# Reordering the prologue of a fused attention and mixer kernel: centroids on ScalarE's queue, argmax ahead of a low part, another low part on GpSimd

## The chip, the cores and the metric

One core of a Trainium2 chip runs the whole program. The metric is the device time of that core in microseconds, the median of the runs shown. The engines are TensorE (PE, with its weight loads PEld), VectorE (DVE), ScalarE (ACT), GpSimd (POOL) and SyncE (SP), which here only issues transfers.

## The reference

The input q, k and v have 2 batches of 8 heads with 768 tokens of 64 values; each head has 16 centroids. Every token of q and of k is assigned to the centroid with the largest product (the first one, if several are equal), and a token attends only to the tokens of its own cluster. Two feed-forward mixers follow.

```python
q_assign = np.argmax(np.einsum('bhsd,hcd->bhsc', q_n, c_n), axis=-1)
k_assign = np.argmax(np.einsum('bhsd,hcd->bhsc', k_n, c_n), axis=-1)
mask = q_assign[:, :, :, None] == k_assign[:, :, None, :]
scores = np.where(mask, scale * np.matmul(q, k.transpose(0, 1, 3, 2)), -1e9)
attn = softmax(scores)
x = np.matmul(attn, v)            # heads joined to (2, 768, 512)
k = np.maximum(xk @ w_k, 0.0)     # xk, xr: x mixed with the token before
x = sigmoid(xr @ w_r) * (k * k @ w_v)
u = x + (np.maximum(x.T @ w_tok1, 0.0) @ w_tok2).T
out = u + np.maximum(u @ w_ch1, 0.0) @ w_ch2
```

## The kernel before, in words

The heads are worked in 8 pairs (2 batches of 4 pairs); head 0 and head 1 below are the two heads of the first pair. For each pair, `loads` (L614) brings q and k of both heads, transposed and doubled over the partitions, in four transfers into four temporary tiles `t0` to `t3`; they are used in turn, so a load of the next pair overwrites the tile that the pair before held in its place. A product is made from two numbers for each value: a high part, rounded to the engine's format (`hi`, L642), and a low part, the value less its high part (`lo`, L650). `hi(e, 0)` and `hi(e, 1)` write the high parts of q and k of head e into `qa` and `ka` on ScalarE; `hi(e, 2)` writes the high part of k once more into `kb`, on GpSimd; `lo(e, 0)` writes the low part of q into `qb` and `lo(e, 1)` the low part of k into the lower half of `ka`. The score of a block of 128 tokens (`score`, L826) is a sum of two parts: part 0 from `qa` and `ka`, and part 1 from `qb` and `kb`. Rows 64 to 79 of `qb` and `kb` hold the cluster mask.

The mask is made so: the centroids are loaded (`cr`, L939), squared and summed on ScalarE (L947), normalised by a chain of small operations on GpSimd and VectorE, transposed on TensorE and copied to `cn` (L967). For the first pair, `sims_head(e)` (L671) forms the similarities of one head on TensorE from `cn` and the raw q and k, `sime_head` (L698) copies them out on ScalarE, `simt_head` (L681) transposes them on TensorE, `first_max(e)` (L738) finds the argmax in five steps on VectorE (L743, L744, L747, L750 and L691, which writes the one-hot rows `oh`), `mask_first` (L771) transposes `oh` on TensorE, and `mask_evac` (L776) writes the mask rows, for q on VectorE (L780) and for k on ScalarE (L782). Then part 1 of the first scores can run, then the row maximum (L844, VectorE), the exponential (L853, ScalarE), transposes and products with v.

Each engine has a queue of its own and executes it in the order in which the program writes the instructions; semaphores between the queues are put in by the framework. Three things set the order around the change. The prologue from L937 to L969 is written out by hand: constants, centroids, loads, and then the branch `n == 0` of `prep_steps` (L784 to L808), whose lines stand in the order in which their instructions are issued. The list that it returns (`first`) holds the steps of the first pair that are left to the planner: `lo(1, 1)` and `hi(1, 2)` on GpSimd, `lo(1, 0)` and the second argmax on VectorE, and others. From there on a planner (`run_plan`, L997) orders the attention of all 8 pairs: each operation has an engine, an assumed duration, its dependencies and a due time; for each engine the ready operation with the smallest sum of start time and 0.29 of the due time is next. Due times come from `want` (L1053), which adds a multiple of a period to `T_FIRST`, the time at which the steady order is assumed to begin; the planner's clocks of the engines start from the same constant:

```python
def want(n, key, j=0.0):
    return T_FIRST + PER * (n + (EARLY.get(n, LATE.get(n - NP, {})).get(key, DUE[key]) + j) / NTASK)

now.update(P=T_FIRST + 0.75, A=T_FIRST + 0.5, D=T_FIRST + 0.65, G=T_FIRST - 2, S=T_FIRST - 6)
```

The planner runs while the program is built; nothing of it is measured at run time. After the attention the mixers run with TensorE as the engine that most work waits for, their weights converted on VectorE and ScalarE beside it.

Of the kernel before, what the change touches and what calls it, by code (L numbers as in the profile page):

```python
# [50 lines left out]
MM512 = 0.2265  # L51
GSTEPS = 18
PER = 23.929
T_FIRST = 11.753
CROSS = 0.117
LAND = 2.1
SWITCH = 0.122
# [241 lines left out]
def f32(ap):  # L299
    return ap.bitcast(F32)  # L300
# [3 lines left out]
def cluster_attention_moe_mixer(ctx: ExitStack, tc, q, k, v, cent, mu_k, mu_r, w_k, w_v, w_r, w1, w2, wc1, wc2, out):  # L304
    nc = tc.nc
# [44 lines left out]
    class Chain:  # L350
# [14 lines left out]
        def step(self, n=1):  # L365
            for _ in range(n):
                e, us, two = self.op[:3]
                t = self.start() + us
                now[e] = t
                if e == "G":  # L370
                    lock[1] = t
                elif two:
                    lock[0] = t
                self.ready = t + LAT
                self.count += 1
                self.op = next(self.gen, None)
                if self.op is None:
                    self.done = True
                    pipe.remove(self)
                    return  # L380
                if len(self.op) > 3:
                    self.due = self.op[3]
# [214 lines left out]
    with ExitStack() as actx:  # L597
# [8 lines left out]
        def copy(eng, dst, src):  # L606
            if eng == "D":
                nc.vector.tensor_copy(dst, src)
            elif eng == "A":
                nc.scalar.activation(dst, src, AF.Copy)  # L610
            else:
                nc.gpsimd.tensor_copy(dst, src)
# [16 lines left out]
        def prep_steps(n):  # L629
# [12 lines left out]
            def hi(e, w):  # L642
                qa, qb, ka, kb = stks[n]
                dst, src = ((qa[:, e], qr[e]), (ka[:, e], kr[e]), (kb[0:D, e], kr[e][0:D]))[w]
                if w == 2 and n and ENG["hi2"] == "S":
                    nc.sync.dma_start(out=f32(dst), in_=f32(ka[0:D, e]))
                else:
                    copy(ENG[f"hi{w}"], dst, src)

            def lo(e, w, eng=None):  # L650
                eng = eng or (nc.vector if ENG[f"lo{w}"] == "D" else nc.gpsimd)
                qa, qb, ka, kb = stks[n]
                if w == 0:
                    dst, src, h = qb[0:D, e], qr[e][0:D], qa[0:D, e]
                else:
                    dst, src, h = ka[D:P, e], kr[e][D:P], ka[D:P, e]
                eng.tensor_tensor(out=dst, in0=src, in1=f32(h), op=ALU.subtract)
# [13 lines left out]
            def sims_head(e):  # L671
                st["ps", e] = ps = banks8[:, (6, 5)[e], 0:HS]
                for hf in range(2):
                    for j, r in ((0, qr), (1, kr)):
                        o = 32 * (2 * hf + j)
                        nc.tensor.matmul(
                            ps[o : o + 32, :], cn[0:D, 2 * p + e, :], r[e][0:D, hf * HS : (hf + 1) * HS],
                            start=True, stop=True,
                        )

            def simt_head(e):  # L681
                ps = banks8[:, (6, 4)[e], 0:HS].rearrange("p (h i a b) -> p h i a b", h=2, i=HT, b=32)
                for i in range(HT):
                    nc.tensor.transpose(
                        ps[:, :, i].rearrange("p h a b -> p h (a b)"), st["sm", e][:, i * P : (i + 1) * P], ident
                    )
                groups = ps.rearrange("p h i a b -> p (h i a) b")
                st["sv", e], st["eq", e] = groups[:, :, 0:NC], groups[:, :, NC:]

            def aoh_head(e):  # L690
                nc.vector.tensor_tensor(  # L691
                    out=ohs.rearrange("p h i a b -> p (h i) a b")[:, :, 2 * e : 2 * e + 2, 0:NC],
                    in0=st["rk", e].rearrange("p (g a) b -> p g a b", a=2),
                    in1=st["m2", e].rearrange("p (g a) -> p g a", a=2).unsqueeze(3).to_broadcast([P, NT, 2, NC]),
                    op=ALU.is_equal,
                )

            def sime_head(e):  # L698
                if e == 0:
                    st["sm"] = sml.tile([P, S], F32, tag="sm", bufs=1, name="sm")  # L700
                st["sm", e] = sm = st["sm"][:, e * HS : (e + 1) * HS]
                nc.scalar.activation(sm, st["ps", e], AF.Copy)
# [35 lines left out]
            def first_max(e):  # L738
                mx = sml.tile([P, HT * 4], F32, tag=f"mx{e}", bufs=1, name="mx")
                st["m2", e] = m2 = sml.tile([P, HT * 4], F32, tag=f"m2{e}", bufs=1, name="m2")  # L740
                st["rk", e] = rk = st["eq", e]
                return [
                    lambda: nc.vector.tensor_reduce(mx, st["sv", e], axis=AX.X, op=ALU.max),  # L743
                    lambda: nc.vector.tensor_tensor(  # L744
                        out=rk, in0=st["sv", e], in1=mx.unsqueeze(2).to_broadcast([P, HT * 4, NC]), op=ALU.is_ge
                    ),
                    lambda: nc.vector.tensor_tensor(  # L747
                        out=rk, in0=rk, in1=rank.unsqueeze(1).to_broadcast([P, HT * 4, NC]), op=ALU.mult
                    ),
                    lambda: nc.vector.tensor_reduce(m2, rk, axis=AX.X, op=ALU.max),  # L750
                    lambda: aoh_head(e),
                ]
# [18 lines left out]
            def mask_first(j, e, at):  # L771
                ps = st["pf", j] = banks8[:, at].bitcast(BF16)[:, 0:S]
                for i in range(NT):
                    nc.tensor.transpose(ps[D : D + 32, i * P : (i + 1) * P], oh[i // HT][:, i % HT, 2 * e + j], identb)
# [8 lines left out]

            alloc()  # L784
            if n == 0:
                hi(0, 0), hi(0, 1)
                sims_head(0)
                fill(FILL[1])
                lo(0, 1, nc.vector)
                sime_head(0), simt_head(0)  # L790
                lo(0, 0, nc.vector)
                sims_head(1)
                hi(1, 1), sime_head(1), hi(1, 0)
                for step in first_max(0):
                    step()
                for i, t in enumerate(tasks[0:2]):
                    score(t, 0, at=2 * i)
                simt_head(1)
                hi(0, 2)
                mask_first(1, 0, 6), mask_first(0, 0, 7)  # L800
                mask_evac(0, 1, 0, S), mask_evac(0, 0, 0, HS)
                return [
                    lambda: lo(1, 1), lambda: lo(1, 0, nc.vector), lambda: hi(1, 2),
                    first_max(1),
                    lambda at: mask_first(0, 1, at), lambda at: mask_first(1, 1, at),
                    lambda: mask_evac(1, 0, 0, HS), lambda: mask_evac(1, 0, HS, S), lambda: mask_evac(1, 1, 0, S),
                    lambda: mask_evac(0, 0, HS, S),
                ]  # L808
# [17 lines left out]
        def score(t, part=None, at=None):  # L826
            n, hf, i, e = t
            qa, qb, ka, kb = stks[n]
            c0 = (hf * HT + i) * P
            if t not in PS_:  # L830
                PS_[t] = banks8[:, at : at + 2]
            ps = PS_[t]
            parts = ((qa, ka, True), (qb[0 : D + NC], kb[0 : D + NC], False))
            for x, y, first in parts if part is None else parts[part : part + 1]:
                for nh in range(2):
                    nc.tensor.matmul(  # L836
                        ps[:, nh, 0:HS], x[:, e, c0 : c0 + P], y[:, e, nh * HS : (nh + 1) * HS],
                        start=first, stop=not first,
                    )
# [96 lines left out]

        cr2 = sml.tile([P, 2, D], F32, tag="cr", bufs=1, name="cr")  # L937
        cr = cr2[:, 0]
        nc.sync.dma_start(cr, cent)  # L939
        loads(0)  # L940
        load_v(0)
        warm = banks8[:, 4, 0:P]
# [19 lines left out]
        def fill(count):  # L962
            for _ in range(count):
                nc.tensor.transpose(warm, ident, ident)

        fill(FILL[0])
        nc.vector.tensor_copy(cn[:, :, 0:NC], pc.rearrange("p (h c) -> p h c", h=H))  # L967

        first = prep_steps(0)  # L969

        NP = len(pairs)
# [81 lines left out]
# [4 lines that stand above are left out]
        prep, score_, max_, exp_, turn_, tp_, ev_, move_, pv_, xe_, parts, load_, mask_dma, load_v_ = ({} for _ in range(14))  # L1057
# [529 lines left out]
```

## Time and profile before

| | us |
|---|---|
| median of 3 runs | 621.73 |
| lowest and highest run | 620.47, 622.57 |
| the profiled execution | 621.98 |
| its span | 620.2 |
| TensorE busy | 606.2 (98%) |
| VectorE busy | 477.2 (77%) |
| ScalarE busy | 356.1 (57%) |
| GpSimd busy | 128.5 (21%) |

The span runs from the first to the last instruction of the profiled execution; the device time has 1.8 us more around it. Busy times are sums over the span, so an engine that is idle half of the time can still be the one that all others wait for in a stretch. The chain of waits goes back from the last instruction: at each step to what released it, or to the instruction before it on its engine; "issue" in it is time in which the engine waited for nothing that the profile shows. The granted clock of TensorE was 0.999 of its full speed.

### The profile page before, as it was taken

The page shows a single profiled execution, that of the slowest core. Times are in us where ns is not written, and L with a number is a line of the kernel's source. Part 1 is how long each engine was busy: PE and PEld are TensorE (multiplying, and loading weights), DVE is VectorE, ACT ScalarE, POOL GpSimd, SP SyncE. Part 2 cuts the span into 40 slices and gives each one's busy share as a digit, 9 for nine tenths or more (in the row PEclk, how much of TensorE's full clock was granted, in tenths as well). Part 3 has the DMA queues.
Part 4 walks back from the last instruction along what each step waited for, and adds up shares of the span by engine and source line. Part 5 has one row for each costly group of instructions (what it writes and reads, how often), then busy time and mean ns, then how long its engine had stood idle before and what let it go on. Part 6 is the DMA issues. An engine that isn't in the chain of part 4 may idle for free.

```text
span 620.2 us, 9514 instructions
## 1 busy us (share of the span) xinstructions
PE 606.2 (98%) x3357; PEld 499.1 (80%) x3357; DVE 477.2 (77%) x850; ACT 356.1 (57%) x677; POOL 128.5 (21%) x181
## 2 busy tenths in 40 slices
PE   8899999999999999999999999999999999999997
PEld 6765757668678568899999998889999899999996
DVE  5999899899898858899869888968986726774113
ACT  4988888889878667967656666134432512332010
POOL 4455744836622541000000000020002000000000
PEclk9999999999999999999999999999999999999999
DMA  8167758659536341344204334143447203300002
GB/s 299 60 203 197 185 172 247 180 177 284 152 90 178 96 137 57 106 136 150 85 0 134 120 121 135 34 103 102 137 137 166 82 23 134 105 34 1 0 2 101
DMA packets 36736, 75.43 MB, mean 122 GB/s; under 512 B 6033, under 2 KB 19345, under 8 KB 36689
## 3 DMA queue, kind: packets, MB, share of 16 engines
q1 hardware_dynamic: 34256, 67.36, 35.9%
q0 software_dynamic: 2432, 7.47, 5.0%
q8 instruction: 26, 0.43, 0.3%
q14 instruction: 22, 0.17, 0.1%
HBM read 48.27 MB, written 3.15 MB: 83 GB/s over the span
## 4 chain that ended last, share of the span: by engine, by line
PE 80%; DVE 9%; DMA 4%; ACT 2%; SPq 2%; issue 2%; POOL 1%; ACTq 0%; DVEq 0%
PE ps L1333 25%; PE ps L1357 24%; PE ps L836 9%; PE ps L925 9%; PE ps L590 5%; PE ps L909 3%; DVE junk L844 3%; DMA uperm<-ublk 2%; DMA t<-k_dram 2%; SPq L1455 1%; PE ps L1413 1%; PE ps L1496 1%; DVE ut L1468 1%; PE ps L666 1%; DVE ublk L1438 1%
## 5 line engine op out<-in xcount | busy, mean ns | idle before, releaser
L1357 PE MATMUL ps<-wu,hl 128*128 128x512 f32 x720 | 170.5, 391 | 0.0
L1357 PEld LDWEIGHTS ps<-wu,hl 128*128 128x128 f32 x720 | 134.6, 188 | 26.8
L1333 PE MATMUL ps<-ut,wu 128*128 128x384 f32 x576 | 104.5, 336 | 0.9 <-DVE ut L1468 0.5
L1333 PEld LDWEIGHTS ps<-ut,wu 128*128 128x128 f32 x576 | 100.9, 188 | 3.5 <-DVE ut L1468 1.0
L844 DVE TENSOR_SCALAR_CACHE_REDUCE junk<-ps 128x768 bf16<-128x768 f32 x96 | 90.1, 938 | 9.3 <-PE ps L836 5.2
L853 ACT ACTIVATE e<-ps,nm 128x768 f32<-128x768 f32 x96 | 86.6, 904 | 18.4 <-DVE junk L844 17.1
L1312 ACT ACTIVATE hl<-ps 128x384 fp32r<-128x384 f32 x48 | 23.4, 490 | 93.8 <-PE ps L1333 93.7
L1314 DVE SCALAR_TENSOR_TENSOR hl<-ps,hl 128x384 fp32r<-128x384 f32 x48 | 26.8, 557 | 60.0 <-ACT hl L1312 59.7
L480 ACT ACTIVATE wu<-g 128x512 fp32r<-128x512 f32 x62 | 39.0, 629 | 56.2 <-DVE g L476 56.1
L1333 PE MATMUL ps<-xmix,wu 128*128 128x384 f32 x384 | 69.7, 336 | 0.7 <-ACT wu L480 0.5
L1333 PEld LDWEIGHTS ps<-xmix,wu 128*128 128x128 f32 x384 | 67.3, 188 | 2.4 <-ACT wu L480 0.8
L836 PE MATMUL ps<-ka,qa 128*128 128x384 f32 x192 | 57.7, 380 | 1.6 <-DVE oh L733 0.8
L1455 POOL DMA_DIRECT2D uperm<-ublk x16 | 7.9, 499 | 228.9 <-ACT h L1400 168.3
L836 PE MATMUL ps<-kb,qb 80*128 80x384 f32 x192 | 49.5, 340 | 1.1 <-DVE qb L780 0.7
L836 PEld LDWEIGHTS ps<-ka,qa 128*128 128x128 f32 x192 | 29.9, 189 | 22.9 <-issue 8.8
L476 DVE SCALAR_TENSOR_TENSOR g<-wu,g 128x512 f32<-128x512 f32 x62 | 42.7, 691 | 6.1 <-ACT wu L468 1.7
L482 DVE TENSOR_TENSOR wu<-g,wu 128x512 fp32r<-128x512 f32 x58 | 40.7, 701 | 8.4 <-ACT wu L480 6.8
L888 DVE STREAM_TRANSPOSE tb<-e 128x768 f32<-128x768 f32 x48 | 46.0, 966 | 0.0
L464 DVE SCALAR_TENSOR_TENSOR g<-wraw,g 128x512 uint32<-128x512 uint32 x62 | 42.8, 690 | 1.2
L470 DVE SCALAR_TENSOR_TENSOR g<-wraw,g 128x512 uint32<-128x512 uint32 x62 | 42.4, 685 | 0.2
L468 ACT ACTIVATE wu<-wraw 128x512 fp32r<-128x512 f32 x62 | 40.3, 661 | 0.0
L909 PE MATMUL ps<-ident,e 128*128 128x128 f32 x288 | 39.5, 273 | 0.4 <-ACT e L853 0.4
(117 smaller groups left out, 856.5 us busy)
## 6 DMA issues: line engine op xcount, KB each, us to landing
wraw<-moe_w_ch_dram SPq DMA_DIRECT2D x34, 512.0 KB, 3.5
ptd<-tb SPq DMA_DIRECT2D x88, 144.0 KB, 3.9
t<-q_dram SPq DMA_DIRECT2D x16, 384.0 KB, 5.3
t<-k_dram SPq DMA_DIRECT2D x16, 384.0 KB, 6.0
ptd<-tb POOLq DMA_DIRECT2D x40, 144.0 KB, 4.3
wraw<-moe_w_k_dram SPq DMA_DIRECT2D x9, 512.0 KB, 3.4
wraw<-moe_w_v_dram SPq DMA_DIRECT2D x9, 512.0 KB, 3.8
v<-v_dram SPq DMA_DIRECT2D x8, 384.0 KB, 3.1
```

Of the source, the lines that this page charges most:

```text
L464: nc.vector.scalar_tensor_tensor(out=g, in0=high, scalar=0xC0000000, in1=g, op0=ALU.bitwise_and, op1=ALU.bitwise_or)
L470: nc.vector.scalar_tensor_tensor(out=g, in0=low, scalar=29, in1=g, op0=ALU.logical_shift_right, op1=ALU.bitwise_or)
L476: nc.vector.scalar_tensor_tensor(out=gf, in0=f32(t[:, 1, :]), scalar=TINY, in1=gf, op0=ALU.is_ge, op1=ALU.mult)
L482: (nc.gpsimd if key[0] == "wr" else nc.vector).tensor_tensor(out=t[:, 1, :], in0=gf, in1=f32(t[:, 0, :]), op=ALU.subtract)
L836: nc.tensor.matmul(ps[:, nh, 0:HS], x[:, e, c0 : c0 + P], y[:, e, nh * HS : (nh + 1) * HS], start=first, stop=not first,)
L844: nc.vector.tensor_scalar(junk, PS_[t][:, :, 0:HS], -SCALE, None, op0=ALU.mult, op1=ALU.min, accum_out=nm)
L853: nc.scalar.activation(et.rearrange("p (a b) -> p a b", a=2), PS_.pop(t)[:, :, 0:HS], AF.Exp, bias=NM_.pop(t), scale=SCALE, accum_out=ss_[ ...
L888: nc.vector.transpose(out=T_[n][:, :, e, :, i, :].rearrange("p j k q -> p k j q"), in_=E_.pop(t).rearrange("p (k j c) -> p k j c", j=4, c=32),
L909: nc.tensor.transpose(ps[:, kk], E_[t][:, kt * P : (kt + 1) * P], ident)
L925: nc.tensor.matmul(o, vts[n][:, e, kt, :], m, start=(kt == 0), stop=(kt == NT - 1))
L1333: nc.tensor.matmul(ps[:, 0:HS], u[:, wl, c, :], xin(xl, c, sl), start=(n == 0), stop=(n == 11))
L1357: nc.tensor.matmul(accs[st], prev[:, xl, st * P : (st + 1) * P], u[:, wl, :], start=(idx == 1 and n == 0), stop=(idx == nf and n == 2),)
```

## The change

The centroids are loaded by ScalarE's queue instead of SP's, where they stood ahead of the first loads of q and k. In the branch for the first pair, the copy `hi(0, 2)` is written next to the other high parts of head 0; the low part of k of head 0 goes from VectorE to GpSimd; the five steps of the first argmax are written ahead of the second head's similarities, and the low part of q of head 0, which stood ahead of them, comes after them, behind the high parts of head 1. The constant `T_FIRST` is lowered from 11.753 to 10.7.

```diff
-T_FIRST = 11.753
+T_FIRST = 10.7
@@
             if n == 0:
-                hi(0, 0), hi(0, 1)
+                hi(0, 0), hi(0, 1), hi(0, 2)
                 sims_head(0)
                 fill(FILL[1])
-                lo(0, 1, nc.vector)
+                lo(0, 1, nc.gpsimd)
                 sime_head(0), simt_head(0)
-                lo(0, 0, nc.vector)
+                for step in first_max(0):
+                    step()
                 sims_head(1)
                 hi(1, 1), sime_head(1), hi(1, 0)
-                for step in first_max(0):
-                    step()
+                lo(0, 0, nc.vector)
                 for i, t in enumerate(tasks[0:2]):
                     score(t, 0, at=2 * i)
                 simt_head(1)
-                hi(0, 2)
                 mask_first(1, 0, 6), mask_first(0, 0, 7)
                 mask_evac(0, 1, 0, S), mask_evac(0, 0, 0, HS)
@@
-        nc.sync.dma_start(cr, cent)
+        nc.scalar.dma_start(cr, cent)
```

## Rows read from the trace of the kernel before

**Rows 1.** Busy time of each engine in three stretches (instructions in brackets).

```profile
core 0: us, PE busy (x) PEld busy (x) DVE busy (x) ACT busy (x) POOL busy (x), PEclk, DMA share, GB/s
13.60:41.00 27.40, 25.39 (x179) 18.62 (x178) 26.92 (x55) 21.97 (x44) 10.25 (x10) 1.00 0.37 128
41.00:53.00 12.00, 11.23 (x85) 9.31 (x85) 11.33 (x26) 11.87 (x24) 11.75 (x13) 1.00 0.75 199
66.00:620.00 554.00, 547.05 (x2950) 457.43 (x2946) 421.74 (x735) 307.23 (x587) 94.82 (x112) 1.00 0.39 113
```

**Rows 2.** The chain of waits in order of time: start, us, what.

```profile
1.63 4.68 DMA t<-k_dram
6.33 0.85 ACT ka L610
7.21 0.96 DVE ka L657
...
9.07 0.35 DVE mx L743
...
9.92 0.38 DVE ps L747
...
12.66 0.95 DVE qb L657
...
15.89 0.38 DVE ps L747
...
54.12 8.52 DMA t<-k_dram
```

**Rows 3.** Timeline, TensorE and VectorE: start, us, engine, line, operation, tiles.

```profile
6.08 1.11 PE L676 MATMUL ps<-t,cn 64*32 64x384 f32 x8
...
7.82 0.55 PE L684 MATMUL ps<-ident,sm 128*128 128x128 f32 x3
...
8.30 0.89 PE L676 MATMUL ps<-t,cn 64*32 64x384 f32 x8
...
9.93 0.49 PE L684 MATMUL ps<-ident,sm 128*128 128x128 f32 x3
...
11.19 0.84 PE L774 MATMUL ps<-identb,oh 128*32 128x128 bf16 x12 [0.77 <-DVE oh L691]
...
12.08 0.56 DVE L780 TENSOR_SCALAR qb<-ps 16x384 fp32r<-16x384 bf16 x1 [0.94 <-PE ps L774]
```

**Rows 4.** Timeline, ScalarE and SP's queue (SPq).

```profile
0.72 1.28 ACT L947 ACT_TABLE_LOAD   x1 [0.72 <-PEq L1577]
...
0.72 0.39 SPq L939 DMA_DIRECT2D cr<-cent_dram  x1
...
2.49 0.26 ACT L947 ACTIVATE csq<-cr 128x64 f32<-128x64 f32 x1 [0.49 <-DMA cr<-cent_dram]
...
9.30 0.33 SPq L620 DMA_DIRECT2D t<-q_dram  x1
```

**Rows 5.** Timeline, GpSimd, and the first reader of pair 1 on TensorE.

```profile
9.31 1.83 POOL L657 TENSOR_TENSOR ka<-t,ka 64x768 fp32r<-64x768 f32 x1 [2.12 <-ACT ka L610]
11.20 0.82 POOL L612 CAST kb<-t 64x768 fp32r<-64x768 f32 x1
18.65 0.82 POOL L612 CAST kb<-t 64x768 fp32r<-64x768 f32 x1 [6.64 <-DMA t<-k_dram]
...
22.72 0.88 PE L666 MATMUL ps<-t,cn 64*32 64x384 f32 x16
```

**Rows 6.** Timeline, GpSimd and VectorE, two places between 214 and 237 us.

```profile
214.54 0.50 POOL L612 COPY rw<-rs 128x384 f32<-128x384 f32 x1
214.63 3.02 DVE L535 SCALAR_TENSOR_TENSOR t<-xT,mu,t 128x768 f32<-128x768 f32 x1 [2.65 <-POOL xmix L544]
215.01 1.82 POOL L544 TENSOR_TENSOR xmix<-t,xmix 128x768 fp32r<-128x768 f32 x1
...
233.63 1.85 POOL L544 TENSOR_TENSOR xmix<-t,xmix 128x768 fp32r<-128x768 f32 x1 [4.57 <-ACT xmix L542]
234.48 1.82 DVE L535 SCALAR_TENSOR_TENSOR t<-xT,mu,t 128x768 f32<-128x768 f32 x1 [2.48 <-ACT t L533]
```

## The prediction, as it was recorded before the changed kernel was run

> **What bounds the kernel now.** I read the table of busy times by stretches first [rows 1]; the reader is to look for the engine that is full in each. From 13.6 to 41 us it is VectorE (26.92 of 27.40 us), from 41 to 53 us it is GpSimd (11.75 of 12.00), then a load of k ends the wait (54.12 + 8.52 us, [rows 2]), and from 66 us on it is TensorE (547.05 of 554.00), so that over most of the kernel only an earlier start is worth anything. That load is issued when GpSimd's stretch is over, so every link of this chain begins with the end of the one before it, and none is tied to a clock. I therefore take a shift of VectorE's work at about 13 us to be carried whole to the end. The change is made wholly ahead of that, so the question is how far VectorE's work from 12.08 us on moves.
>
> Ahead of 12 us I read the chain of waits in order of time [rows 2]. It runs: k of head 0 (issued 1.63, landed 6.31), ScalarE's high part of k until 7.18, VectorE's low part of k (7.21, 0.96 us), VectorE's low part of q (0.95, as the one at 12.66), first argmax from 9.07, TensorE's mask transposes at 11.19 [rows 3], and at 12.66 VectorE's low part of q of head 1. The reader is to see that first argmax at 9.07 waits for nothing but VectorE's own queue: the similarities it reads are transposed by 8.37 (7.82 + 0.55, [rows 3]). And after it VectorE idles for 0.94 us before the mask's evacuation at 12.08 [rows 3].
>
> **The assumed time (T_FIRST).** All clocks of the planner except the zero of its bookkeeping queue N are set from T_FIRST, every due time is T_FIRST plus a constant, and the choice compares start + 0.29 due, so lowering the constant adds the same amount to all candidates. The initial zeros (free banks, locks) lie below every start either way. I cost it at nothing: the written order stays. Were that wrong, there is no row for it; it is a rival below.
>
> **Centroids by ScalarE's queue.** SP issues the centroids at 0.72 and k of head 0 two slots later at 1.63 [rows 2, 4]; one slot is (1.63 - 0.72) / 2 = 0.45 us. All of SP's later issues move up by 0.45. I take it that k lands 0.45 earlier, at 5.86; the bounds are 0 (all engines of the DMA already full) and 0.45. A greater gain is excluded, since nothing else leaves that queue. On ScalarE the issue takes a slot of 0.39 and pushes the table load from 0.72 to 1.11, so it ends at 2.39; the square of the centroids started at 2.49, when they had landed, 0.49 us after the table load [rows 4]. So 0.10 us of room is left. The centroids now share the engines with q: I add 0.1 us; at least 0 (same issue time), at most 1.28 (below). First similarities then start at 6.08 + 0.1 = 6.18 and no longer wait for k inside: they take 0.89 like those of head 1, not 1.11 [rows 3], and end at 7.07 instead of 7.19.
>
> What the rows show of the table load is 1.28 us and a next instruction 0.49 us behind it, released by a transfer. The Trainium skill (ScalarE: Activation LUTs, What ACT_TABLE_LOAD costs) speaks against the move: it adds a drain of 1.38 us to every switch, 2.66 us in all. By that, as an estimate, the square would start at 1.11 + 2.66 = 3.77, 1.28 late. The trace doesn't agree: 0.49 us after the load the square ran.
>
> **Argmax ahead of low q, low k to GpSimd.** VectorE loses 0.96 + 0.95 us in front of the first argmax, which can start 0.05 us after the transposes, as the mask's evacuation did (12.03 to 12.08, [rows 3]). Similarities' end to argmax was 8.42 - 7.19 = 1.23; so 7.07 + 1.23 = 8.30, 0.77 earlier than 9.07. It takes 2.12 with the hand-off to TensorE (9.07 to 11.19), so low q is ready at 10.38 and the masks' transposes move to 10.42. GpSimd's subtraction beside it costs nothing: a step of it took 0.38 us with GpSimd busy and 0.38 without (9.92 and 15.89, [rows 2]; GpSimd busy from 9.31 to 11.14, [rows 5]). TensorE, in order, was done with all ahead of those transposes at 10.42 [rows 3]. The evacuation could start at 12.08 - 0.77 = 11.31.
>
> GpSimd's low part of k takes 1.83 us [rows 5] where VectorE's took 0.96: 6.76 (7.21 - 0.45) to 8.59. Its reader, the first half of the scores, stands on TensorE behind the similarities of head 1, which end at 9.19 [rows 3]: 0.6 us of cover, 0.15 if k doesn't land earlier. The copy of k to kb is only written earlier in the program; it is GpSimd's next work either way, so nothing.
>
> Low q now lies in VectorE's gap before the evacuation, and it meets GpSimd's low part of k of head 1, 8.86 to 10.69 (9.31 - 0.45). Both engines there read two operands from SBUF, and [rows 6] show what such a pair does: a VectorE operation that began at 234.48 beside a GpSimd one ran 1.82 us and ended 0.82 us after it. So low q waits from 10.38 to 10.69, and ends at about 10.69 + 0.8 = 11.49 (that VectorE gets in there and not GpSimd's next operation is a choice; rival 1 is the other end). The evacuation follows at 11.52: 0.56 earlier than 12.08. Then GpSimd's copy of k of head 1 (0.82, [rows 5]), which had waited in its turn, holds VectorE's low q of head 1 from 12.10 to about 12.27. It started at 12.66; what is left is **0.39 us earlier**.
>
> **Queued behind.** SP's first load of pair 1 overwrites q of head 0, so it waits for low q: 11.6 instead of 9.30 [rows 4], and three loads stand behind it. They had landed when GpSimd copied the k at 18.65, and TensorE reads them at 22.72 [rows 5]: some 4 us of cover, and the third and fourth were held anyway by low q of head 1. Nothing, as long as the cover lasts.
>
> **Sum.** -0.39 us. The profiled execution took 621.98 us (span 620.2, 1.8 around it), 0.25 above the median; on its own time that is 621.6, on the median 621.73 it is 621.3. A measurement can tell 0.3% from no change, 1.87 us here.
>
> **Rivals.**
> 1. The copy goes first. When low part of k ends, GpSimd's copy is ready too. [Rows 6] have one such contest: VectorE's operation of 214.63 waited through the copy at 214.54 and also through the subtraction that followed it at 215.01, and ran 3.02 us. Then low q waits until 10.75 + 0.82 = 11.57, ends at 12.37, and the evacuation starts at 12.40, **0.32 later** than before: 622.05, slower. With k landing no earlier it is 11.20 + 0.82 + 0.8 + 0.03 = 12.85, 0.77 later, 622.5. It decides from the point where both wait at 10.69. Against it: there a subtraction followed with no gap; here there was a gap of 0.06 (9.31 + 1.83 to 11.20), in which VectorE may get in.
> 2. No meeting at all (the low q is not held, or GpSimd's is later): low q ends at 11.33, evacuation at 11.36, 0.72 earlier: 621.0. For it: only the form of the operations differs from [rows 6]; against: both have two SBUF operands.
> 3. ScalarE's queue is serial: the table load stands ahead of the issue. The centroids are issued at 2.00 and everything of theirs is 1.28 later: similarities 7.36 to 8.25, argmax 9.48 to 11.56, low q until 12.52, evacuation 12.55, 0.47 later: 622.2. The row can't show which stands first, as both were at 0.72 on different queues. By the drain of the Trainium skill (ScalarE: Activation LUTs, What ACT_TABLE_LOAD costs) the time would be the same.
> 4. The change does something else than it says: the order of the steady part changes with T_FIRST after all, or a load's contention carries a different wait. The one wait of 8.52 us [rows 2] is the size such a thing can reach; I price it at a quarter of that, 2 us, either way, by choice.
>
> **How the numbers follow.** Forecast 0.40, rival 1 0.30, rival 2 0.10, rival 3 0.10, rival 4 0.10. The cases of the first four lie between 621.0 and 622.5, all within 0.3%. Single runs scatter from 620.47 to 622.57, so I let the range reach 0.9 us below the lowest and 0.3 above the highest case: 620.1 to 622.8, which leaves out rival 4 and some scatter. Faster by over 0.3%: half of rival 4 and 0.02 of scatter, 0.07; slower 0.05; within 0.88. The sign below that bound is close: forecast and rival 2 are faster, 0.50; rivals 1 and 3 slower, 0.40.
>
> **What would show it.** Right: the square of the centroids at about 2.6, q issued at 0.72, argmax at about 8.3, low q stretched to 1.1 us, evacuation near 11.5, GpSimd's copy after it, and the order of instructions beyond 14 us as before. Wrong: low q stretched to 2 us (rival 1), the square near 3.7 (rival 3), evacuation at 11.36 (rival 2), or a steady part whose length from 13 us to the end differs by over 0.5 us.

## The result, and the profile after

The changed kernel takes 626.37 us (median of 6 runs, 625.97 to 626.68); the kernel before took 621.14 us beside it (6 runs, 620.47 to 622.57). The ratio is 1.0085, 95% interval 1.0073 to 1.0098: the change makes the kernel slower, by 5.2 us between the medians. The profiled execution took 626.62 us with a span of 624.8 (before: 621.98 and 620.2). One run of e7 below (1212.19 us) and one of e8 (1003.85 us) were in a slow state; the medians and ratios given here leave them out.

The chain of waits in order of time, of the changed kernel (start, us, what), shows a link at its beginning that the one before [rows 2] doesn't have:

```profile
0.72 4.25 DMA cr<-cent_dram
59.38 7.89 DMA t<-k_dram
...
207.10 7.91 PE ps L924 x48
...
232.94 20.68 PE ps L590 x90
```

The same two stretches of TensorE in the chain of the kernel before:

```profile
202.02 7.92 PE ps L925 x48
...
227.84 20.68 PE ps L590 x90
```

The reader is to see that the load of the centroids now takes 4.25 us, and that from the load of k (54.12 before, [rows 2]) to the mixers all stands about 5.1 us later: 5.26, 5.08 and 5.10. So the whole loss is made ahead of 54 us. The timeline of ScalarE and of SP's queue (SPq) in the changed kernel shows where it begins:

```profile
0.72 0.41 ACTq L938 DMA_DIRECT2D cr<-cent_dram  x1
1.16 1.28 ACT L946 ACT_TABLE_LOAD   x1 [1.16 <-PEq L1576]
4.99 0.26 ACT L946 ACTIVATE csq<-cr 128x64 f32<-128x64 f32 x1 [2.55 <-DMA cr<-cent_dram]
...
0.73 0.38 SPq L620 DMA_DIRECT2D t<-q_dram  x1
1.17 0.42 SPq L620 DMA_DIRECT2D t<-k_dram  x1
```

The centroids are issued at 0.72, as before. But q now goes out in the same moment and k 0.44 us behind it. The square waits for the transfer until 4.99; it ran at 2.49 before [rows 4]. The timeline of TensorE and VectorE tells what follows:

```profile
1.35 3.72 PE L943 MATMUL ps<-ident 128*128 128x128 f32 x20 [1.35 <-POOL ident masks.py:199]
7.82 0.48 PE L959 MATMUL ps<-ident,cr 128*128 128x128 f32 x1 [2.75 <-DVE cr L957]
8.87 1.50 PE L676 MATMUL ps<-t,cn 64*32 64x384 f32 x8
11.43 0.85 PE L684 MATMUL ps<-ident,sm 128*128 128x128 f32 x3
...
12.38 0.36 DVE L743 TENSOR_REDUCE mx<-ps 128x12 f32<-128x192 f32 x1 [3.75 <-PE ps L684]
14.38 0.94 DVE L657 TENSOR_TENSOR qb<-t,qa 64x768 fp32r<-64x768 f32 x1
...
17.35 0.56 DVE L780 TENSOR_SCALAR qb<-ps 16x384 fp32r<-16x384 bf16 x1 [2.03 <-PE ps L774]
```

TensorE ends its first transposes at 5.07 and waits 2.75 us for the normalised centroids. After that wait its work is slow: eight similarities take 1.50 us (0.89 and 1.11 before, [rows 3]), three transposes 0.85 (0.55). The first argmax starts at 12.38 (9.07, [rows 2]), the evacuation at 17.35 (12.08, [rows 3]): 5.27 us late. The busy times by stretches name the reason. Behind the five engines' busy times stand the granted clock of TensorE, the DMA share and GB/s:

```profile
core 0: us, PE busy (x) PEld busy (x) DVE busy (x) ACT busy (x) POOL busy (x), PEclk, DMA share, GB/s
5.00:6.00 1.00, 0.07 (x1) 0.00 (x0) 0.00 (x0) 1.00 (x4) 0.51 (x1) 1.00 1.03 347
6.00:7.00 1.00, 0.00 (x0) 0.00 (x0) 0.69 (x4) 0.80 (x2) 1.00 (x18) 1.00 0.94 332
7.00:8.00 1.00, 0.18 (x1) 0.18 (x2) 0.67 (x3) 0.00 (x0) 0.83 (x12) 0.76 0.99 381
10.00:17.00 7.00, 7.00 (x38) 4.71 (x35) 2.66 (x6) 2.73 (x5) 3.31 (x3) 0.50 0.67 239
17.00:18.00 1.00, 0.32 (x3) 0.05 (x1) 0.62 (x2) 0.51 (x1) 0.00 (x0) 0.62 0.72 252
18.00:19.00 1.00, 0.95 (x6) 0.94 (x7) 0.97 (x2) 0.00 (x0) 0.00 (x0) 1.00 0.92 366
```

After TensorE's idle time the granted clock falls from 1.00 to 0.50, that is from 2.4 to 1.2 GHz, and stays there from 8 to 17 us. The argmax is 3.31 us late and the evacuation 5.27: the rest is lost between them, while TensorE works at half speed.

### The profile page after: what moved, and what is told of

It reads as the page before. It is cut to its first block, busy times and chain, and to the rows that moved or that the text cites. A ratio compares the mean times of both kernels' runs of the same rounds, so it can differ in the third digit from the quotient of the medians.

```text
span 624.8 us, 9513 instructions
## 1 busy us (share of the span) xinstructions
PE 609.8 (98%) x3357; PEld 500.9 (80%) x3357; DVE 476.6 (76%) x849; ACT 355.8 (57%) x677; POOL 130.4 (21%) x182
## 4 chain that ended last, share of the span: by engine, by line
PE 81%; DVE 9%; DMA 4%; ACT 2%; SPq 1%; issue 1%; POOL 1%; ACTq 0%; DVEq 0%; POOLq 0%
PE ps L1332 25%; PE ps L1356 24%; PE ps L835 10%; PE ps L924 9%; PE ps L590 5%; PE ps L908 3%; DVE junk L843 3%; DMA uperm<-ublk 2%; SPq L1454 1%; PE ps L1412 1%; DMA t<-k_dram 1%; PE ps L1495 1%; DVE ut L1467 1%; PE ps L666 1%; DMA cr<-cent_dram 1%
## 5 line engine op out<-in xcount | busy, mean ns | idle before, releaser
L464 DVE SCALAR_TENSOR_TENSOR g<-wraw,g 128x512 uint32<-128x512 uint32 x62 | 42.7, 689 | 1.2
```

Source lines behind the costliest of these rows:

```text
L464: nc.vector.scalar_tensor_tensor(out=g, in0=high, scalar=0xC0000000, in1=g, op0=ALU.bitwise_and, op1=ALU.bitwise_or)
```

## The experiments

Each ratio is to the kernel before in the same series, whose medians were 620.95, 620.89, 621.05 and 620.83 us. To follow a shift through a trace I used one row that recurs 96 times, the row maximum (L844 before), and took the start of the n-th one less the start of the n-th in the trace of before:

| kernel | 1st (13.92) | 21st (52.20) | 25th (64.46) | 31st (75.65) | 49th (111.54) | 95th (202.51) |
|---|---|---|---|---|---|---|
| after | +5.27 | +5.28 | +4.63 | +4.84 | +4.87 | +5.07 |
| e1, centroids on SP | -0.27 | -0.25 | -0.90 | -0.68 | -0.64 | -0.47 |
| e4, longer warm-up | +2.16 | +2.18 | +2.19 | +2.19 | +2.18 | +2.36 |
| e5, load ahead on SP | -0.51 | -0.51 | -1.46 | +0.76 | +0.82 | +1.04 |
| e9, before, steps late | -0.64 | -0.65 | -1.25 | -1.26 | +0.16 | +0.13 |
| e12, before, steps early | -0.07 | -0.05 | -0.46 | -0.46 | -0.48 | -0.56 |
| e13, e1, steps early | +0.22 | +0.23 | -0.32 | -0.32 | -0.32 | -0.33 |
| e14, e5, steps early | -0.53 | -0.51 | -0.92 | -0.89 | -0.90 | -0.91 |

### Which part of the change costs the time

**e1: the change, with the centroids back on SP's queue.**

```diff
-        nc.scalar.dma_start(cr, cent)
+        nc.sync.dma_start(cr, cent)
```

> The changed kernel with the centroids back on SP's queue; argmax ahead of low q, low k on GpSimd and the lower T_FIRST stay. Theory A (the whole loss comes from the centroids landing at 4.97 instead of 2.45 us): the square runs near 2.5 us, TensorE keeps its 2.4 GHz level, first argmax starts near 8.4 us, the evacuation of the mask (VectorE, L780) starts between 11.3 and 12.0, and the time is 0.1 to 0.8 us below the kernel before. Rival B (the moves of low q and low k cost by the meeting of VectorE and GpSimd): the evacuation starts at 12.4 to 12.9 and the time is 0.3 to 0.8 us above before. Rival C (the moves are most of the loss): still over 2 us above before.

621.43 us, ratio 1.0007 (0.9997 to 1.0016): the loss is gone, and no gain is left; the 0.1 to 0.8 us below before that theory A expected didn't come. Its timeline:

```profile
2.53 0.26 ACT L946 ACTIVATE csq<-cr 128x64 f32<-128x64 f32 x1 [0.53 <-DMA cr<-cent_dram]
...
8.79 0.36 DVE L743 TENSOR_REDUCE mx<-ps 128x12 f32<-128x192 f32 x1 [2.38 <-PE ps L684]
10.79 0.94 DVE L657 TENSOR_TENSOR qb<-t,qa 64x768 fp32r<-64x768 f32 x1
11.81 0.56 DVE L780 TENSOR_SCALAR qb<-ps 16x384 fp32r<-16x384 bf16 x1
```

The square is back at 2.53. The low part of q begins when GpSimd's low part of k of head 1 is done, and the evacuation is 0.27 us ahead of the 12.08 of before [rows 3].

**e2: the kernel before, with only that line changed the other way.**

```diff
-        nc.sync.dma_start(cr, cent)
+        nc.scalar.dma_start(cr, cent)
```

> The kernel before with the centroids alone on ScalarE's queue. Theory A: the centroids land near 5 us, TensorE idles from about 5.2 to 7.8 us and falls to 1.2 GHz, and the time is about 5 us above before, as in the changed kernel, since VectorE's two low parts lie in the long wait. Rival C: clearly less than half of the loss, under 2.5 us.

626.31 us, ratio 1.0081 (1.0065 to 1.0096): this one line makes the whole loss. The square ran at 5.01, the evacuation at 17.38. Its trace has one trap, in the timeline and in the busy times by stretches:

```profile
8.89 1.50 PE L676 MATMUL ps<-t,cn 64*32 64x384 f32 x8
...
10.00:17.00 7.00, 7.00 (x38) 4.68 (x35) 2.44 (x6) 2.71 (x5) 2.62 (x2) 1.00 0.82 330
```

The matmuls take the 1.50 us of the slow clock, yet the record of the granted clock shows 1.00. The durations decide; the record can lack a fall. The runs of the change fit this: two of the six have a mean granted clock of 0.992 and four 1.000, and both kinds take 626.0 to 626.7 us.

**e3: the kernel before, with only `T_FIRST` lowered to 10.7.**

> The kernel before with T_FIRST lowered alone. The planner's argument says that no instruction moves: no difference, within 0.3%. The rival (another steady order): a difference of over 1 us, and another order beyond 14 us.

620.96 us, ratio 0.9999 (0.9987 to 1.0011): nothing. TensorE, VectorE, ScalarE and GpSimd execute the same instructions in the same order as in the kernel before.

### Queue, or order of the bytes

**e8: the kernel before, with the centroids second on SP's own queue.** They are issued behind the first q.

```diff
                     lst.append(t)
+                    if cr is not None and e == 0 and lst is qr:
+                        nc.sync.dma_start(cr, cent)
```

> The kernel before with the centroids as the second load on SP's queue, behind the first q. Theory A1 (what counts is which bytes are ahead, not the queue): they land later than 2.45 us, about with the first q at 4.2 to 5, the square near 4.5 to 5.1, TensorE idles and falls to 1.2 GHz, 3.5 to 5.5 us above before. Rival A2 (SP's queue is fast, ScalarE's slow): the square by 3.2 us, under 1 us above before.

625.11 us (three runs), ratio 1.0067 (1.0052 to 1.0083). ScalarE's queue isn't used for a load here, and some four fifths of the loss are made all the same. The square, at 4.15, is a little earlier than theory A1 expected (4.5 to 5.1). The timeline:

```profile
1.17 0.42 SPq L623 DMA_DIRECT2D cr<-cent_dram  x1
...
4.15 0.26 ACT L948 ACTIVATE csq<-cr 128x64 f32<-128x64 f32 x1 [2.14 <-DMA cr<-cent_dram]
...
6.98 0.33 PE L961 MATMUL ps<-ident,cr 128*128 128x128 f32 x1 [1.65 <-DVE cr L959]
...
10.83 1.51 PE L678 MATMUL ps<-t,cn 64*32 64x384 f32 x8
```

The wait of TensorE is 1.65 us, and again its later work runs at half speed (1.51 us for eight similarities).

**e5: the change, with a load ahead of q on SP's queue.** The centroids are loaded twice; nothing reads the second copy, which only holds q back by one slot.

```diff
         nc.scalar.dma_start(cr, cent)
+        nc.sync.dma_start(sml.tile([P, D], F32, tag="cd", bufs=1, name="cd"), cent)
         loads(0)
```

> The changed kernel (centroids on ScalarE's queue), but SP first issues a second, unused load of the centroids, so that its first load of q starts one slot later, at 1.17 instead of 0.73 us as before. Theory A1 (the centroids lost their head start on the loads of q and k): ScalarE's load of the centroids lands near 2.5 us, the square starts at 2.5 to 2.9, and the time is within 0.3% of the kernel before. Rival A2 (ScalarE's queue is slow in itself, as its first transfer): it still lands at 4 us or later, and the time stays 4 to 5.5 us above before.

622.15 us, ratio 1.0019 (1.0010 to 1.0028). The timeline of its head, and of the places that matter later:

```profile
2.65 0.26 ACT L947 ACTIVATE csq<-cr 128x64 f32<-128x64 f32 x1 [0.21 <-DMA cr<-cent_dram]
...
8.37 0.36 DVE L743 TENSOR_REDUCE mx<-ps 128x12 f32<-128x192 f32 x1 [2.23 <-PE ps L684]
10.37 1.17 DVE L657 TENSOR_TENSOR qb<-t,qa 64x768 fp32r<-64x768 f32 x1
11.57 0.56 DVE L780 TENSOR_SCALAR qb<-ps 16x384 fp32r<-16x384 bf16 x1
...
64.98 1.60 DVE L1176 TENSOR_SCALAR omu<-mu 128x8 f32<-128x8 f32 x1
...
66.96 1.83 POOL L657 TENSOR_TENSOR ka<-t,ka 64x768 fp32r<-64x768 f32 x1 [0.42 <-ACT ka L610]
66.97 2.37 DVE L464 SCALAR_TENSOR_TENSOR g<-wraw,g 128x512 uint32<-128x512 uint32 x1
```

Issued by ScalarE at 0.72 with q only at 1.16, the centroids are there at 2.65. That is 1.93 us after the issue, against 1.77 us by SP's queue in the kernel before [rows 4]. So ScalarE's queue is about as quick as SP's; what was lost is the 0.44 us by which the small load was ahead of the large ones. The Trainium skill (DMA: Bandwidth & Descriptors, Issuing engines are not separate DMA queues) says that transfers issued by different engines run on the same DMA engines and interleave, and that issuing on several saves only the sequencer's time. By that rule a move to another queue buys one issue slot, and no priority. e2, e5 and e8 agree.

### How much of the loss is the clock

**e4: the change, with 34 first transposes instead of 20,** so that TensorE is busy until the centroids are ready.

```diff
-WARM = 20
+WARM = 34
```

> The changed kernel with 34 instead of 20 transposes of the identity at the start, so that TensorE is busy until about 7.8 us, when the centroids' transpose can run. Theory A with two costs (late landing 2.5 us, and the fall of TensorE's clock as the rest): the granted clock stays at 2.4 GHz, similarities of head 0 take 0.9 instead of 1.5 us, the evacuation starts near 13.8 us and the time is 1.5 to 2.5 us above before. Rival (the clock doesn't matter, all comes from the landing and what hangs on it): within 0.7 us of the changed kernel, 5 us above before.

624.13 us, ratio 1.0043 (1.0028 to 1.0057): some 2 us less than the change. The timeline:

```profile
7.71 0.33 PE L959 MATMUL ps<-ident,cr 128*128 128x128 f32 x1 [0.27 <-DVE cr L957]
8.47 0.85 PE L676 MATMUL ps<-t,cn 64*32 64x384 f32 x8
...
12.58 0.82 POOL L612 CAST kb<-t 64x768 fp32r<-64x768 f32 x1
12.60 1.61 DVE L657 TENSOR_TENSOR qb<-t,qa 64x768 fp32r<-64x768 f32 x1
14.24 0.56 DVE L780 TENSOR_SCALAR qb<-ps 16x384 fp32r<-16x384 bf16 x1
```

The load is as late as in the change (square at 4.88), the matmuls run at full speed (0.85 against 1.50), and the evacuation stands at 14.24 instead of 17.35. So of the 5.27 us in the traces, 3.11 go with the slow clock and 2.16 stay. The 2.16 aren't the late load alone: the low part of q, just ahead of the evacuation, met GpSimd's copy here and took 1.61 us, where it took 0.94 in the change. By the medians, each against the kernel before in its own series, 3.18 of 5.23 us stay (624.13 - 620.95, 626.37 - 621.14), which leaves 2.05 to the clock. The clock's part is therefore 2 to 3 us, and no run here fixes it closer.

### Why the reordering brings nothing

**e6: the kernel before, with the low part of q ahead of that of k on VectorE.**

```diff
-                lo(0, 1, nc.vector)
+                lo(0, 0, nc.vector), lo(0, 1, nc.vector)
                 sime_head(0), simt_head(0)
-                lo(0, 0, nc.vector)
```

> The kernel before with one thing changed: VectorE's low q of head 0 is written ahead of its low k of head 0 (q lands 1.6 us earlier than k, and VectorE idles from 5.98 to 7.21), so both are done when the similarities are transposed, and nothing goes to GpSimd. Theory: low q about 6.0 to 6.95, low k 7.2 to 8.2, first argmax at 8.4, evacuation 11.4 to 11.6 with no operation of GpSimd to wait for, and the time 0.3 to 0.7 us below before. Rival (a shift of VectorE's work at 12 us isn't carried to the end, or TensorE's start scatters as much): evacuation early but time within 0.2 us of before.

620.76 us, ratio 1.0002 (0.9992 to 1.0011): nothing, and the expected evacuation at 11.4 to 11.6 came at 12.06. In its trace the argmax, at 9.04, waits 0.77 us for TensorE, whose first transposes took 4.53 us in that execution (4.10 in that of before).

**e7: e1 with the low part of k on VectorE again.** Only the argmax is then ahead.

```diff
-                lo(0, 1, nc.gpsimd)
+                lo(0, 1, nc.vector)
```

> The changed kernel with the centroids on SP's queue and low k of head 0 back on VectorE, so of the moves only the argmax ahead of low q is left (and the lower T_FIRST). Theory: low k on VectorE is done near 8.2 us, before the argmax can start, so GpSimd's taking it over is worth nothing: evacuation within 0.3 us of the kernel with the centroids on SP's queue, 11.5 to 12.1. Rival: low k on VectorE holds the argmax up, evacuation later than 12.1.

621.31 us, ratio 1.0009 (1.0000 to 1.0018), against e1's 621.43: by the medians it makes no difference where the low part of k is formed. The trace missed the expectation: the argmax starts at 8.81 (8.79 in e1), but the evacuation at 12.33 instead of 11.5 to 12.1. The trace gives another reason than the low part of k of head 0: k of head 1 landed later in this execution (ScalarE's high part of it starts at 8.68, 7.98 in e1), and so GpSimd's low part of it held VectorE's low part of q.

**e9, e10, e11: the meeting of 64 to 69 us moved away,** in the kernel before, in e1 and in e5. In e5's table line the shift of -1.46 at 64 us turns into +0.76 by 75 us. Between them, as e5's last three lines above show, two steps of VectorE met GpSimd's subtractions (64.72 to 66.54 and 66.96 to 68.79): `omu` (1 - mu, L1176) took 1.60 us and L464 2.37. In the kernel before they ran in 0.68 and 0.69 us; these are the rows of the second there (timeline):

```profile
67.47 0.69 DVE L464 SCALAR_TENSOR_TENSOR g<-wraw,g 128x512 uint32<-128x512 uint32 x1
...
68.42 1.84 POOL L657 TENSOR_TENSOR ka<-t,ka 64x768 fp32r<-64x768 f32 x1 [1.33 <-ACT ka L610]
```

It ended at 68.16, 0.26 us ahead of GpSimd's start. In the three kernels the first gate weight's two steps are issued just ahead of its third, some 21 us later, and `omu` is computed on ScalarE (`exponent` and `sign` are the steps of L460 and L464 as functions):

```diff
+            late = key == ("wr", 0)
...
+            if not late:
+                exponent()
             yield "D", 0.62, True
+            if not late:
+                sign()
             yield "A", 0.56, False
...
             yield "D", 0.62, True
+            if late:
+                exponent(), sign()
...
-        Op("D", 0.1, want(1, "f0"), lambda: nc.vector.tensor_scalar(omu, mu, -1.0, 1.0, op0=ALU.mult, op1=ALU.add), [lm])
+        Op("D", 0.1, want(1, "f0"), lambda: nc.scalar.activation(omu.rearrange("p a k -> p (a k)"), mu.rearrange("p a k -> p (a k)"), AF.Copy, scale=-1.0, bias=1.0), [lm])
```

> The kernel before, with VectorE's two steps on the first gate weight (L460, L464) issued later, just ahead of its third, and the small 1 - mu (L1176) moved to ScalarE, so that VectorE has no such work between 64 and 69 us. Theory (an early head is given back where VectorE meets GpSimd at 65 to 69 us): in the kernel before that meeting costs little (0.68 and 0.69 us a step), so this gives 0 to 1 us: 619.9 to 621. Rival (the meeting is not where the head's shift went): nothing, 620.9.

> The change with the centroids on SP's queue again, and the same two edits as the run before it. Theory: its evacuation is 0.27 us earlier and its load of k some 0.5 us earlier, and nothing gives that back at 65 to 69 us; so it is 0.3 to 1 us below the kernel before with those edits, and below the 621.43 it had without them. Rival: equal to the kernel before with those edits, or still 621.4.

> The change with a first, unused load of the centroids on SP's queue (the centroids are loaded twice), and the same two edits. Without them it lost 1.3 us although its load of k was 0.5 us earlier than before. Theory: the loss was made at 65 to 69 us; it is gone, and 0.3 to 1.5 us come in beside: 619.4 to 620.6. Rival: the loss was made elsewhere, and it stays at 622.2.

622.34, 622.75 and 622.37 us; ratios 1.0021 (1.0012 to 1.0030), 1.0029 (1.0018 to 1.0040) and 1.0022 (1.0012 to 1.0033). All three expectations failed: the edit made even the kernel before slower. Its timeline in e9 shows a reason:

```profile
90.78 4.33 POOL L669 TENSOR_TENSOR ka<-t,ka 64x768 fp32r<-64x768 f32 x2
91.23 2.21 DVE L468 SCALAR_TENSOR_TENSOR g<-wraw,g 128x512 uint32<-128x512 uint32 x1
```

And in the kernel before, at the same place:

```profile
91.30 0.71 DVE L464 SCALAR_TENSOR_TENSOR g<-wraw,g 128x512 uint32<-128x512 uint32 x1
...
91.92 1.83 POOL L657 TENSOR_TENSOR ka<-t,ka 64x768 fp32r<-64x768 f32 x1
```

In the kernel before, the next weight's step is done ahead of GpSimd's subtraction. In e9 GpSimd is 1.1 us earlier, but the moved steps held VectorE, so that this step starts at 91.23, inside the subtraction, and takes 2.21 us. The table shows it: -1.26 at the 31st row maximum, +0.16 at the 49th. The meeting was moved, not removed. That this is the whole loss isn't shown: the execution traced took 621.47 us, 0.9 below e9's median.

**e12, e13, e14: the steps early.** `omu` (on VectorE again) and the two steps are issued ahead of the 25th row maximum, where VectorE waits for TensorE anyway; in the kernel before, in e1 and in e5.

```diff
         def rowmax(t):
+            nth[0] += 1
+            if nth[0] == 25:
+                for fn in ahead:
+                    fn()
...
+        for o in (oms, conv[0][0], conv[0][1]):
+            ahead.append(o.fn)
+            o.fn = lambda: None
```

> The kernel before, with three VectorE steps (1 - mu and the first two on the first gate weight) issued ahead of the row maximum of 64.46 us, where VectorE waits 2.38 us for TensorE and GpSimd has no subtraction. In the last three runs the steps at 66 to 69 us were moved to 88 us, and a later weight step met GpSimd there and took 2.21 us. Theory (the meetings decide what of a shift lasts): neither meeting is made; about 1.2 us comes off the wait at 66 to 68 us, and the time is 0.6 to 1.3 us below before, 619.7 to 620.4. Rival (the next wait takes it back, as another load or GpSimd is late): 620.9 to 621.1.

> The change with the centroids on SP's queue again, and the same three steps early. Theory: as the run before it, and the head's reordering adds its 0.2 to 0.5 us, since nothing between 64 and 100 us takes it back: 619.3 to 620.0, 0.2 to 0.5 below the run before it. Rival: the reordering is worth nothing at all: equal to the run before it within 0.2 us.

> The change with the unused load of the centroids on SP's queue (the centroids are loaded twice), and the same three steps early. It lost 1.3 us without them. Theory: the loss was the meeting of 66.96 us; it is gone: 619.3 to 620.2. Rival: it stays above before, 621.5 to 622.4.

620.69, 620.85 and 621.59 us; ratios 0.9993 (0.9984 to 1.0002), 1.0002 (0.9994 to 1.0011) and 1.0012 (1.0000 to 1.0024). The timeline of e14:

```profile
61.98 0.69 DVE L464 SCALAR_TENSOR_TENSOR g<-wraw,g 128x512 uint32<-128x512 uint32 x1
63.54 0.96 DVE L849 TENSOR_SCALAR_CACHE_REDUCE junk<-ps 128x768 bf16<-128x768 f32 x1 [0.87 <-PE ps L835]
...
201.60 0.92 DVE L849 TENSOR_SCALAR_CACHE_REDUCE junk<-ps 128x768 bf16<-128x768 f32 x1
```

In these three traces the step takes 0.69 us and the shift at 64 us is carried to 202 us within 0.1 (-0.92 to -0.91 in e14). So in the profiled executions the meeting is what took e5's lead. In the medians the theory does not hold up, and all three expectations of a gain failed: e12 can't be told from before, e13 and e1 neither, and e14, though 0.6 us under e5 (another series, and the intervals overlap), is still not below before. In e14 the single runs go from 620.67 to 623.43, and the profiled execution, 620.73, is one of the lowest. Where the others lose is not shown by any trace, and stays open. No version beats the kernel before.

**The head differs from execution to execution too.** e1, e13 and e10 have the same prologue, yet their mask evacuation starts at 11.81, 12.30 and 12.50: 0.27 us ahead of the kernel before, and 0.22 and 0.42 behind it. The timeline of e13:

```profile
8.71 0.84 ACT L610 ACTIVATE ka<-t 128x768 fp32r<-128x768 f32 x1 [0.77 <-DMA t<-k_dram]
...
9.63 1.83 POOL L657 TENSOR_TENSOR ka<-t,ka 64x768 fp32r<-64x768 f32 x1 [1.16 <-ACT ka L610]
...
10.65 1.62 DVE L657 TENSOR_TENSOR qb<-t,qa 64x768 fp32r<-64x768 f32 x1
```

ScalarE waits until 8.71 for k of head 1, which e1 used at 7.98. So GpSimd's low part of it ends at 11.46 (10.72 in e1), and VectorE's low part of q, begun at 10.65, lasts until after that. In e1, e3, e10, e13 and e14 this load is issued at 2.58 or 2.59, and its reader on ScalarE starts between 7.96 (e14) and 9.22 (e3). What the reordering is worth over many executions can't be read from a trace of each.

## Why the prediction was wrong

**Centroids by ScalarE's queue: the step that failed.** The forecast was 621.3 us, in a range of 620.1 to 622.8; 626.37 were measured. The step is: "I add 0.1 us; at least 0 (same issue time), at most 1.28 (below)." The load landed 2.50 us later (square at 4.99 against 2.49 in [rows 4]). The bound was taken from the issue time and the table load alone. It should have come from what the load would share the DMA engines with: its 1.77 us (0.72 to 2.49, [rows 4]) were measured with a slot of 0.45 us ahead of q, and no row of before showed it beside q. The nearest row for that was the load of k at 1.63, 4.68 us [rows 2]; the centroids' 4.25 us is of that size.

**A missing term: the clock.** Nothing in the sum said what TensorE does when the centroids are late. It waited 2.75 us, its clock fell, and 2 to 3 of the 5.2 us came with that (e4). The rivals that moved the landing (rival 3, +0.47) priced a delay as a plain shift. Rival 3 was also wrong in its mechanism: the issue went out at 0.72 and the table load stood behind it, at 1.16. Rival 4 named load contention, but its 2 us were less than half of what was measured.

**The table load.** Right: pushed to 1.16, 1.28 us long. In e5 the square ran 0.21 us after its end (2.44 to 2.65), so a drain of 1.38 us, which the Trainium skill (ScalarE: Activation LUTs, What ACT_TABLE_LOAD costs) adds, is not in this trace either.

**The earlier k: not shown.** The sum let k of head 0 land 0.45 us earlier, at 5.86, since it is issued a slot earlier. But in e1, e5, e6, e7, e13 and e14 it is issued at 1.63, as before, and GpSimd's copy reads it between 5.53 and 6.07 (6.37 before). The gain of a slot is within what this landing scatters.

**The head's working.** Where the centroids come in time, it holds, but not in every execution. e5 against the prediction: argmax 8.37 (8.30), low q 10.37 to 11.54 (10.38 to 11.49), evacuation 11.57 (11.52), low q of head 1 at 12.15 (12.27); e14 agrees (evacuation at 11.55). In e1 the argmax is 0.49 us later than forecast, as TensorE's first transposes took 4.53 us, and in e10 and e13 the late k of head 1 turns the gain into a loss. The meeting with GpSimd was there in e5, e10, e13 and e14, and VectorE got in ahead of the copy. In e4 both were ready near 12.5 and the copy went first, as rival 1 had it: low q took 1.61 us. The Trainium skill (SBUF — State Buffer, Who interferes with whom) says that a VectorE instruction with two SBUF inputs contends with a GpSimd one that reads SBUF, and of VectorE's two-port modes that whoever issues first keeps the shared ports to its end while the other blocks. The lengths agree with both (1.17 and 1.61 us against 0.94, 2.37 against 0.69); which of two waiting engines is next, it doesn't say, and the runs show either.

**Low part of k on GpSimd, and T_FIRST.** Right: by the medians both cost nothing (e7 against e1, and e3). From the first row maximum on, the engines execute the same order in the change as in the kernel before, so the other steady order of rival 4 is ruled out.

**Queued behind.** Right: the first load of pair 1 was issued at 11.69 in e5 (11.6), and the shift after it stayed as it was up to 52 us.

**A shift at 13 us is carried whole to the end.** Right in the traces as far as 52 us: the first and the 21st row maximum agree within 0.03 us in every line of the table. From there it holds only roughly. The load of k took 7.58 us in e5, 7.89 in the change and 8.52 before [rows 2], and a VectorE step that slides into a subtraction of GpSimd costs 1.5 to 1.7 us at once. A delay of 5 us passed almost whole; a gain of 0.39 us is no larger than these, and than the start itself. TensorE's first 20 transposes took 3.72 us in one execution and 4.53 in another: they follow each other by 0.21 us at first and then by 0.11, at half the speed and at the full one, from about the 13th on in the change, from about the 17th on before, and not within the 20 in e1. And e9, whose head is that of before, has its first row maximum 0.64 us earlier. So the -0.39 us of the sum is in no median: e1 has 1.0007.

## What to carry to other kernels

A small load that stands at the head of a dependency chain is best issued ahead of the large ones, on whichever queue; when an issue is moved to another engine, ask which bytes now leave together with it. When a change can make TensorE wait, price its slower work after the wait beside the wait itself. And where two engines are ordered to miss each other by a few tenths of a us, compare a gain of that size upstream with what the landings of loads and the start of TensorE scatter: here the mask's evacuation stood at 11.81 in one trace and at 12.50 in another of the same prologue (e1, e10), and a gain that was made could end in a collision (e5).

## What was not expected of the hardware

- A load of 128 x 64 values issued with q took 4.25 us. With 0.44 us of start it was used 1.93 us after its issue (e5, 0.72 to 2.65).
- After 1.65 us of idle time (e8) and after 2.75 us (the change) TensorE's matmuls ran at half speed; with a wait of 0.27 us (e4) they didn't.
- The record of the granted clock showed 1.00 in a stretch in which the matmuls ran at half speed (e2), and in the change at 2 to 3 us, where transposes follow each other by 0.21 us instead of 0.11.
- A VectorE step on 128 x 8 values took 0.13 us alone (e14) and 1.60 beside a subtraction of GpSimd (e5).
- A load issued at 2.58 to 2.59 us was first used by ScalarE at 7.96 us in one execution and at 9.22 in another (e14, e3).
